# Splits of weights through a PSUM bank, one bank less for layer 2, and one quadrant kept in PSUM

## The chip, the cores and the metric

The kernel runs on one core of one Trainium2 chip. The metric is device time in microseconds of one execution; the kernel before was timed in three runs. The engines are named as in the profile: PE (TensorE, matmuls), PEld (its weight loads), DVE (VectorE), ACT (ScalarE), POOL (GpSimd), SP (SyncE, which issues most DMAs).

## The reference, cut to what matters

```
x = retention(q, k, v)            # scores * decay mask, times v; 4 x 576 tokens = 2304, 512 wide
for e in range(4):                # first mixture: every token through every expert
    out1 += p[:, e] * (relu(x @ w1[e]) @ w2[e])        # w1: 512x1024, w2: 1024x512
e_idx = argmax(out1 @ w_gate)     # second mixture: one of 8 experts per token
out[t] = gate[t] * sigmoid(out1[t] @ w_output_gate)[e_idx] * (relu(out1[t] @ w1s[e_idx]) @ w2s[e_idx])
```

All matrix products are done with pairs of float16 numbers: each float32 operand is split into `hi` (the float16 value) and `lo` (what is left, also as float16), and three products hi·hi, hi·lo, lo·hi are summed in PSUM.

## The kernel before, in words

**Splitting.** `split(raw, hi, lo, scale)` (lines 191 to 193) makes such a pair from a float32 tile in SBUF: ACT writes `hi` from `raw` (L192), then DVE computes `raw*scale - hi` into `lo` (L193). DVE so reads two tiles in SBUF, `raw` and `hi`. Three kinds of tiles go through it in the middle of the program: the first mixture's weights of experts 1 to 3 (`put`, tiles `wr` to `wm_a`, `wm_b`, `wm_c`), the staged pieces of the second mixture's weights (`s_split`, tiles `sr` to `s`, written back to DRAM for later), and rows of the result for the gate (`g1_rows`, tile `xr`). The splits of the opening and those whose source is already in PSUM use the same function.

**Expert 0** (`e = 0`, 18 to 268 us of the trace): nine blocks of 256 tokens. In a block, four units of layer 1 (`l1_first`, PSUM tag `h`) and four of layer 2 (`l2`, PSUM tag `o`) run, with steps of the retention (`at_hook`) and one staged piece (`s_hook`) between them. `x_keep` splits mixed token tiles at the end of a block: `hi` by ACT (L349), `lo` by DVE (L350).

**Experts 1 to 3** (268 to 816 us) use a product scheme with seven instead of eight quarter products (matrices cut in quadrants and mixed first). A block has seven layer-1 units (products 1, 5, 6, 2, 3, 7, 4; 24 matmuls each, L523) that alternate with seven layer-2 units of the block before it (12 matmuls each, L608). The mixing of the weights is done by POOL (`mix`, L438), each mixed quarter is then split by `put`; the lower halves `lo` of the mixed activations are done by POOL too (L542).

In layer 1, PSUM banks `x` (tag `h`), `y` and `q` hold running sums. Product 5 is copied from `q` to an SBUF tile `s5` by ACT (L564); later DVE adds a running sum to it in place (L583, in `m7`), and this tile is the source of two mixes (L546) and of the quadrant "22" (`keep`, L481 and L482). In the traces' names the tile `s5` is shown as `s`.

In layer 2, products 1, 6, 7 and 4 go through one bank `X` (tag `x2`), each followed by an `add` on DVE into the accumulator `acc` (L616, `acc<-px`). Products 1 and 6 are summed on top of each other in `X`, as are all four: unit 6 can start only after the `add` of unit 1 has read `X`. Product 5 starts a second bank `v` (`acc<-pv` 128x256), which 2 and 3 then fill. The order of the products is the list `ORDER2`. Before, `X` has two buffers and `v` is taken from the pool `ps_o` (tag `o`), so a block's `X` doesn't wait for the block before.

**What sets the order on an engine.** Each engine works off its own list in order. The lists are made by a scheduler when the program is built, from the order of the code and its own estimate; `tc.issue_after` keeps a split behind the last `keep`. `w_plan` says after which units a weight step is done and `s_plan` after which units a staged piece.

The last stage (816 to 1042 us) is the second mixture: gathered rows, matmuls of L1019 and L1036, scattered rows.

Of the kernel before, what the change touches and what calls it, by code (L numbers as in the profile page):

```python
# [43 lines left out]
HOOKS = {0: 1, 2: 1}, {0: 1, 2: 1, 3: 1, 5: 1}  # L44
W1_AT = {24: 0, 25: 2, 26: 1, 27: 3}
ORDER1 = (1, 5, 6, 2, 3, 7, 4)
ORDER2 = (1, 5, 6, 2, 7, 3, 4)
W1_POS = (
    {2: ("a", 8), 0: ("a", 9), 1: ("a", 10), 3: ("a", 11), 5: ("c", 0), 4: ("c", 1), 6: ("c", 2)},
    {c: ("a", c) for c in range(7)},  # L50
# [79 lines left out]
def kernel(  # L130
# [60 lines left out]
    def split(raw, hi, lo, scale):  # L191
        act.activation(out=hi, in_=raw, func=ACTF.Copy, scale=scale)  # L192
        dve.scalar_tensor_tensor(out=lo, in0=raw, scalar=scale, in1=hi, op0=ALU.mult, op1=ALU.subtract)  # L193

    def w_parts(r, first, second):
        for i in range(2):
# [148 lines left out]
    def x_keep(b):  # L345
        m = xfs.pop(b)
        for i in range(2):
            hi, lo = [xcs[b][:, a, 4 + 2 * i:6 + 2 * i] for a in range(2)]
            act.activation(out=hi, in_=m[:, i], func=ACTF.Copy)  # L349
            dve.tensor_tensor(out=lo, in0=m[:, i], in1=hi, op=ALU.subtract)  # L350
        dst = xcd[b * 128:(b + 1) * 128]
        sp.dma_start(out=dst[:, :, 0:2], in_=xcs[b][:, :, 0:2])
        pace["sp"] = sp.dma_start(out=dst[:, :, 3:], in_=xcs[b][:, :, 3:])
# [75 lines left out]
    def put(e, n, k, i, c):  # L429
        t = wt[e][n][c]  # L430
        if n:
            t = t[:, 2 * k:2 * k + 2]
            split(quarter(e, n, k, i), t[:, :, 0], t[:, :, 1], S_W)
        else:
            split(quarter(e, n, k, i), t[:, k, 0], t[:, k, 1], S_W)

    def mix(e, n, k, to, x, y, op):
        pace["pool"] = pool.tensor_tensor(out=quarter(e, n, k, to), in0=quarter(e, n, k, x), in1=quarter(e, n, k, y), op=op)  # L438
# [71 lines left out]
    def l1_mixed(e, b):  # L510
# [49 lines left out]
        def m5():  # L560
            q = t["q"] = bank("q", later["mix"])
            mm(q, 5, True)
            t["s"] = sb("s5", 2)
            act.activation(out=t["s"], in_=q, func=ACTF.Copy)  # L564

        def m6():
# [12 lines left out]

        def m7():  # L580
            mm(t["x"], 7)
            s5 = t["s"]
            dve.tensor_tensor(out=s5, in0=t["x"], in1=s5, op=ALU.add)  # L583
            mixed("s1", s5, t["r"], ALU.add)
            mixed("s2", s5, t["s3"], ALU.subtract)
            keep(s5, op_of("22"))

        def m4():
            mm(t["x"], 4)
# [6 lines left out]
    def l2_mixed(e, b):  # L596

        o, w = ops[e, b], wt[e][1]
        t = {}
        X = later["mix"].tile([128, 512], F32, tag="x2", name="px2", bufs=2)[:, 0:256]  # L600
        names = {1: ("11", 0), 5: ("s1", 1), 6: ("s2", 2), 2: ("12", 3), 7: ("s3", 4), 3: ("s4", 5), 4: ("22", 6)}

        def mm(out, m, first):
            a, c = names[m]
            n = 0
            for k in range(4):
                for u, v in TERMS:
                    pe.matmul(  # L608
                        out, lhsT=o[a][:, v, k], rhs=w[c][:, k, u], start=(first and n == 0), stop=(n == 11),
                        skip_group_check=True,  # L610
                    )
                    n += 1

        def add(i, c0, c1, src):
            a = acc[:, b * TB + i, c0:c1]
            dve.scalar_tensor_tensor(  # L616
                out=a, in0=src, scalar=p_sb[:, b * TB + i, e:e + 1], in1=a, op0=ALU.mult, op1=ALU.add
            )

        def go(m):  # L620
            if m in (1, 6, 7, 4):
                mm(X, m, m == 1)
                add({1: 0, 6: 0, 7: 1, 4: 1}[m], *{1: (0, 256), 6: (256, 512), 7: (256, 512), 4: (0, 256)}[m], X)
            elif m == 5:
                t["v"] = ps_o[0].tile([128, 2, 256], F32, tag="o", name="pv")
                mm(t["v"][:, 1], 5, True)
                add(1, 256, 512, t["v"][:, 1])
            elif m == 2:
                mm(t["v"][:, 0], 2, False)
            else:  # L630
                mm(t["v"][:, 1], 3, False)
                add(0, 0, 512, t["v"].rearrange("p a d -> p (a d)"))

        return [lambda m=m: go(m) for m in ORDER2]

# [34 lines left out]
    def s_split(i):  # L670
        e, j = divmod(i, 16)
        t = s16_p.tile([128, 2, 512], F16, tag="s16", name="s16")
        split(stage.pop(i), t[:, 0], t[:, 1], S_W)
        if j < 8:
            k, c = divmod(j, 2)
            return w1d[e * 128:(e + 1) * 128, k, :, 512 * c:512 * c + 512], t
        return w2d[e * 128:(e + 1) * 128, j - 8], t
# [28 lines left out]
    def g1_rows(t, pl):  # L706

        xr = pl.tile([128, 2, DM], F16, tag="xr", name="xr")
        split(acc[:, t, 0:DM], xr[:, 0], xr[:, 1], S_X1)
        x1h[t] = xr  # L710

    def g1_turn(t, pl):
# [487 lines left out]

    def s_plan(e, b, u):
        if e == 0:
            if 1 <= b < 8:
                s_hook()
        elif b >= 2 or (e, b) == (1, 1):
            if u in ((1, 5, 8) if b % 2 else (1, 3, 6, 8)):
                s_hook()
        elif b == 1 and u in (6, 8):
            s_hook()
# [38 lines left out]
    for e in range(E1):  # L1248
        for b in range(NB + (e == E1 - 1)):
# [11 lines left out]
                gp.append(ctx.enter_context(tc.tile_pool(name="gp", bufs=2)))  # L1261
            for u, unit in enumerate(units):
                unit()
                if (e, b, u) == (0, NB - 1, 0):
                    with tc.issue_after(pace["sp"].ins):
                        x_load(0, sp)
# [137 lines left out]
```

## Time and profile before

| | us |
|---|---|
| median of 3 runs (lowest, highest) | 1045.91 (1044.99, 1050.87) |
| profiled execution, its own time | 1044.05 |
| span of its trace, first to last instruction | 1042.2 |
| PE busy in the span | 984.2 |
| DVE busy | 616.8 |
| ACT busy | 394.2 |
| POOL busy | 391.5 |

The table is read from the top: the profiled execution has its own time, and what is worked out from its trace is set against that; the span is 1.85 us shorter. PE is busy 94% of the span, so what other engines do matters where PE waits for them. The program has stages with different loads; a mean over the whole span hides that.

### The profile page before, as it was taken

The numbers are of one execution on the slowest core, as the hardware profiler recorded it, in microseconds if no ns is written. First come the engines' busy times: TensorE is split into PE (matmuls) and PEld (weight loads), VectorE is DVE, ScalarE is ACT, GpSimd is POOL, SyncE is SP. The second block draws the span as 40 slices with busy tenths as digits, with TensorE's granted clock in tenths as the row PEclk, the third lists the DMA queues.
The fourth block names the chain that finished last, engine by engine and source line by source line (L and its number), as shares of the span: only waits on it lengthen the run. The fifth ranks groups of instructions, "written<-read, shape, count | busy, mean of one in ns | idle before, by whom it ended". The sixth has DMA issues, their size and how long they took to land. (4 is left out here: it accounts for less than half of the span.)

```text
span 1042.2 us, 30436 instructions
## 1 busy us (share of the span) xinstructions
PE 984.2 (94%) x13075; PEld 819.2 (79%) x13075; DVE 616.8 (59%) x1171; ACT 394.2 (38%) x729; POOL 391.5 (38%) x391
## 2 busy tenths in 40 slices
PE   6899999899998999899899999999999999999995
PEld 5566666566798999899899998898888677777773
DVE  5455444675767877866877687888877512112111
ACT  4234333544533544444445354434432222222221
POOL 3433333644435544533544373423423121121211
PEclk9999999999999999989999999999999999999998
DMA  9778887668363655535464622687436425372691
GB/s 349 215 243 273 266 272 255 222 196 275 121 183 115 178 171 165 148 117 158 120 211 138 204 86 78 177 188 205 128 77 226 175 108 211 125 299 80 262 393 73
DMA packets 94956, 195.10 MB, mean 187 GB/s; under 512 B 21278, under 2 KB 42782, under 8 KB 91744
## 3 DMA queue, kind: packets, MB, share of 16 engines
q1 hardware_dynamic: 84400, 154.35, 44.7%
q0 software_dynamic: 10416, 38.76, 12.3%
q8 instruction: 104, 1.70, 0.7%
q14 instruction: 36, 0.29, 0.1%
HBM read 184.78 MB, written 51.81 MB: 227 GB/s over the span
## 5 line engine op out<-in xcount | busy, mean ns | idle before, releaser
L608 PEld LDWEIGHTS <-op 128*128 128x128 f16 x2268 | 216.0, 99 | 35.6 <-POOL wr L438 10.0
L542 POOL TENSOR_TENSOR op<-sm,op 128x512 f16<-128x512 f32 x108 | 141.9, 1324 | 247.8 <-ACT op L541 244.7
L523 PEld LDWEIGHTS <-wm_a 128*128 128x128 f16 x2592 | 155.3, 98 | 11.9 <-issue 9.0
L193 DVE SCALAR_TENSOR_TENSOR s<-sr,s 128x512 f16<-128x512 f32 x128 | 110.4, 874 | 33.9 <-ACT s L192 33.6
L1029 DVE SCALAR_TENSOR_TENSOR h_s<-p_h,h_s 128x512 f16<-128x512 f32 x40 | 27.6, 690 | 158.4 <-ACT h_s L1028 158.4
L1019 PEld LDWEIGHTS <-wm_a 128*128 128x128 f16 x1920 | 108.9, 98 | 4.2
L1019 PE MATMUL p_h<-x_s,wm_a 128*128 128x128 f16 x1920 | 110.9, 219 | 0.0
L495 PE MATMUL ph<-xc,wm_a 128*128 128x256 f16 (+1 forms) x960 | 101.9, 264 | 8.6 <-POOL xc L335 4.1
L541 ACT ACTIVATE op<-sm 128x512 f16<-128x512 f32 x108 | 67.2, 629 | 100.2 <-DVE sm L546 100.2
L495 PEld LDWEIGHTS <-wm_a 128*128 128x128 f16 x960 | 86.0, 99 | 21.2 <-issue 9.9
L523 PE MATMUL ph<-xc,wm_a 128*128 128x128 f16 x1512 | 94.8, 219 | 8.3 <-DVE s L583 8.3
L646 PE MATMUL po<-wm_a,ht 128*128 128x512 f16 x432 | 96.4, 379 | 1.1 <-DVE xf L331 1.1
L192 ACT ACTIVATE s<-sr 128x512 f16<-128x512 f32 x128 | 77.5, 622 | 47.2 <-DMA w1d<-s 22.7
L438 POOL TENSOR_TENSOR wr<-wr 128x512 f32<-128x512 f32 x48 | 71.5, 1501 | 45.3 <-DVE wm_a L193 29.0
L1036 PEld LDWEIGHTS <-h_s 128*128 128x128 f16 x480 | 46.7, 98 | 52.3 <-DVE h_s L1029 0.7
L1036 PE MATMUL p_y<-wm_b,h_s 128*128 128x512 f16 x372 | 83.9, 379 | 0.5 <-DVE h_s L1029 0.5
L608 PE MATMUL px<-wm_a,op 128*128 128x256 f16 x648 | 79.7, 272 | 2.8 <-DVE acc L616 2.8
L646 PEld LDWEIGHTS <-ht 128*128 128x128 f16 x432 | 40.9, 98 | 49.1 <-DVE xf L331 1.3
L523 PEld LDWEIGHTS <-wm_b 128*128 128x128 f16 x1296 | 76.7, 98 | 1.2
L1039 POOL DMA_INDIRECT out_dram<-y_s,sidxm x17 | 17.3, 1018 | 146.8 <-ACT y_s L1038 138.1
L193 DVE SCALAR_TENSOR_TENSOR wm_a<-wr,wm_a 128x512 f16<-128x512 f32 x62 | 68.0, 1119 | 0.1
L608 PE MATMUL pv<-wm_a,op 128*128 128x256 f16 x540 | 66.5, 273 | 1.2 <-DVE xs L193 0.6
(185 smaller groups left out, 1473.4 us busy)
## 6 DMA issues: line engine op xcount, KB each, us to landing
wm_a<-w1d SPq DMA_DIRECT2D x20, 2048.0 KB
wm_b<-w2d SPq DMA_DIRECT2D x10, 2048.0 KB
wr<-in_w_dram SPq DMA_DIRECT2D x32, 512.0 KB
sr<-in_w1s_dram SPq DMA_DIRECT2D x64, 256.0 KB
w1d<-s SPq DMA_DIRECT2D x64, 256.0 KB
sr<-in_w2s_dram SPq DMA_DIRECT2D x64, 256.0 KB
w2d<-s SPq DMA_DIRECT2D x64, 256.0 KB
xc<-xcd POOLq DMA_DIRECT2D x25, 640.0 KB, 6.1
```

Of the source, the lines that this page charges most:

```text
L192: act.activation(out=hi, in_=raw, func=ACTF.Copy, scale=scale)
L193: dve.scalar_tensor_tensor(out=lo, in0=raw, scalar=scale, in1=hi, op0=ALU.mult, op1=ALU.subtract)
L438: pace["pool"] = pool.tensor_tensor(out=quarter(e, n, k, to), in0=quarter(e, n, k, x), in1=quarter(e, n, k, y), op=op)
L495: pe.matmul(ph[:, i, h0:h1], lhsT=w[:, k, u, f * 128:(f + 1) * 128], rhs=x[:, v, k // 2 + 2 * h0:k // 2 + 2 * h1 - 1:2, k % 2], start=(n = ...
L523: pe.matmul(bank[:, i], lhsT=w[:, k, u, 128 * i:128 * i + 128], rhs=x[:, v, d, k], start=(first and i == 0 and n == 0), stop=(n == 5), ski ...
L541: act.activation(out=hi, in_=s, func=ACTF.Copy)
L542: pool.tensor_tensor(out=lo, in0=s, in1=hi, op=ALU.subtract)
L608: pe.matmul(out, lhsT=o[a][:, v, k], rhs=w[c][:, k, u], start=(first and n == 0), stop=(n == 11), skip_group_check=True,)
L646: pe.matmul(po, lhsT=hts[k // 2][:, x, k % 2, i * 128:(i + 1) * 128], rhs=w[:, k, y], start=(k == 0 and n == 0), stop=(k == KF - 1 and n = ...
L1019: pe.matmul(ph[:, j], lhsT=w[k][:, x, f * 128:(f + 1) * 128], rhs=xs[:, y, k], start=(n == 0), stop=(n == 3 * KD - 1),)
L1029: dve.scalar_tensor_tensor(out=lo, in0=ph, scalar=0.0, in1=hi, op0=ALU.max, op1=ALU.subtract)
L1036: pe.matmul(po, lhsT=h[:, a, k], rhs=w[k][:, b], start=(n == 0), stop=(n == 3 * KF - 1))
```

## The change

Splits of weights, staged pieces and gate rows get a new function `split_z`: ACT copies the scaled source to a bank in PSUM, ACT writes `hi` from that bank, and DVE subtracts `hi` from the bank. That is one more instruction on ACT for each of 224 splits (by the lists of instructions); DVE's instruction now reads one tile in PSUM and one in SBUF. The bank is taken from tag `o` or, in expert 0 behind the layer-1 units, from tag `h`. For that, layer 2 frees a bank: `X` has one buffer, `v` one of its own, and `ORDER2` starts with 5 instead of 1. The sum of `m7` is written to the bank `q` instead of to `s5`, which becomes single. `x_keep`'s subtraction moves from DVE to POOL. `s_plan` puts seven instead of eight pieces in a block of expert 0, and four in every later block instead of three and four by turns.

```
-ORDER2 = (1, 5, 6, 2, 7, 3, 4)
+ORDER2 = (5, 1, 6, 2, 7, 3, 4)
...
+    def split_z(raw, hi, lo, scale):
+        z = z_at["bank"]().tile([128, 512], F32, tag=z_at["tag"], name="pz")
+        if len(raw.shape) == 3:
+            z = z.rearrange("p (k d) -> p k d", k=raw.shape[1])
+        act.activation(out=z, in_=raw, func=ACTF.Copy, scale=scale)
+        act.activation(out=hi, in_=z, func=ACTF.Copy)
+        dve.tensor_tensor(out=lo, in0=z, in1=hi, op=ALU.subtract)
+
+    def z_from(first):
+        z_at["bank"], z_at["tag"] = ((lambda: ps), "h") if first else ((lambda: ps_o[0]), "o")
...
             act.activation(out=hi, in_=m[:, i], func=ACTF.Copy)
-            dve.tensor_tensor(out=lo, in0=m[:, i], in1=hi, op=ALU.subtract)
+            pool.tensor_tensor(out=lo, in0=m[:, i], in1=hi, op=ALU.subtract)
...
-            split(quarter(e, n, k, i), t[:, :, 0], t[:, :, 1], S_W)
+            split_z(quarter(e, n, k, i), t[:, :, 0], t[:, :, 1], S_W)
         else:
-            split(quarter(e, n, k, i), t[:, k, 0], t[:, k, 1], S_W)
+            split_z(quarter(e, n, k, i), t[:, k, 0], t[:, k, 1], S_W)
...
-            t["s"] = sb("s5", 2)
+            t["s"] = sb("s5", 1)
...
             mm(t["x"], 7)
-            s5 = t["s"]
-            dve.tensor_tensor(out=s5, in0=t["x"], in1=s5, op=ALU.add)
-            mixed("s1", s5, t["r"], ALU.add)
-            mixed("s2", s5, t["s3"], ALU.subtract)
-            keep(s5, op_of("22"))
+            q = t["q"]
+            dve.tensor_tensor(out=q, in0=t["x"], in1=t["s"], op=ALU.add)
+            mixed("s1", q, t["r"], ALU.add)
+            mixed("s2", q, t["s3"], ALU.subtract)
+            keep(q, op_of("22"))
...
-        X = later["mix"].tile([128, 512], F32, tag="x2", name="px2", bufs=2)[:, 0:256]
+        X = later["mix"].tile([128, 512], F32, tag="x2", name="px2")[:, 0:256]
...
-                t["v"] = ps_o[0].tile([128, 2, 256], F32, tag="o", name="pv")
+                t["v"] = later["mix"].tile([128, 2, 256], F32, tag="v", name="pv")
...
-        split(stage.pop(i), t[:, 0], t[:, 1], S_W)
+        split_z(stage.pop(i), t[:, 0], t[:, 1], S_W)
...
-        split(acc[:, t, 0:DM], xr[:, 0], xr[:, 1], S_X1)
+        split_z(acc[:, t, 0:DM], xr[:, 0], xr[:, 1], S_X1)
...
         if e == 0:
-            if 1 <= b < 8:
+            if 1 <= b < 8 and u < 7:
                 s_hook()
         elif b >= 2 or (e, b) == (1, 1):
-            if u in ((1, 5, 8) if b % 2 else (1, 3, 6, 8)):
+            if u in (1, 3, 6, 8):
                 s_hook()
...
                 unit()
+                z_from(e == 0 and (b == 0 or u >= 4))
```

**First place: DVE, start of expert 2's first block.** These are DVE's rows before, from the `add` of layer-2 unit 4 of one block to the `add` of unit 6 of the next; `px` with a new number is the new block's `X`.

```order
L616 SCALAR_TENSOR_TENSOR acc<-px_6519,p_sb,acc 128x256
L193 SCALAR_TENSOR_TENSOR wm_c<-wr,wm_c 128x2x256 x2
L193 SCALAR_TENSOR_TENSOR wm_a<-wr,wm_a 128x2x256
L616 SCALAR_TENSOR_TENSOR acc<-px_6855,p_sb,acc 128x256
L193 SCALAR_TENSOR_TENSOR wm_a<-wr,wm_a 128x2x256 x3
L616 SCALAR_TENSOR_TENSOR acc<-pv,p_sb,acc 128x256
L568 TENSOR_TENSOR pq<-ph,s_6930 128x512
L616 SCALAR_TENSOR_TENSOR acc<-px_6855,p_sb,acc 128x256
```

And these are the same stretch of DVE's list in the changed kernel.

```order
L629 SCALAR_TENSOR_TENSOR acc<-px_6735,p_sb,acc 128x256
L203 TENSOR_TENSOR wm_c<-pz,wm_c 128x2x256
L629 SCALAR_TENSOR_TENSOR acc<-pv,p_sb,acc 128x256
L203 TENSOR_TENSOR wm_c<-pz,wm_c 128x2x256
L203 TENSOR_TENSOR wm_a<-pz,wm_a 128x2x256
L629 SCALAR_TENSOR_TENSOR acc<-px_7083,p_sb,acc 128x256
L203 TENSOR_TENSOR wm_a<-pz,wm_a 128x2x256 x2
L581 TENSOR_TENSOR pq<-ph,s_7163 128x512
L203 TENSOR_TENSOR wm_a<-pz,wm_a 128x2x256
L629 SCALAR_TENSOR_TENSOR acc<-px_7083,p_sb,acc 128x256
```

The weight subtractions now read `pz`; the `add` of `pv` (product 5) comes first, and that of `px` (product 1), for which unit 6 waits, is second. Between the two adds stand two subtractions where there were three.

**Second place: ACT, expert 1's fifth block.** Before, ACT's list from the `hi` of quadrant "22" to the copy of product 5:

```order
L481 ACTIVATE op<-s_5274 128x512
L481 ACTIVATE op<-ph 128x512
L192 ACTIVATE wm_a<-wr 128x512
L192 ACTIVATE s_5578<-sr 128x512
L192 ACTIVATE wm_a<-wr 128x512
L192 ACTIVATE s_5666<-sr 128x512
L541 ACTIVATE op<-sm 128x512
L558 ACTIVATE py<-ph 128x512
L564 ACTIVATE s_5606<-pq 128x512
```

In the changed kernel, expert 1's fifth block, from and to the same two:

```order
L494 ACTIVATE op<-pq 128x512
L201 ACTIVATE pz<-wr 128x512
L494 ACTIVATE op<-ph 128x512
L202 ACTIVATE wm_a<-pz 128x512
L201 ACTIVATE pz<-sr 128x512
L202 ACTIVATE s_5399<-pz 128x512
L201 ACTIVATE pz<-wr 128x512
L571 ACTIVATE py<-ph 128x512
L554 ACTIVATE op<-sm 128x512
L202 ACTIVATE wm_a<-pz 128x512
L201 ACTIVATE pz<-sr 128x512
L202 ACTIVATE s_5451<-pz 128x512
L577 ACTIVATE s_5429<-pq 128x512
```

Each `hi` has a copy to `pz` ahead of it, and four more instructions stand between the two ends.

**Third place: DVE in a block of expert 3, where the gate's small work runs too.** Before, from the `add` of product 4 of one block to that of product 5 of the next (`xr` is a gate row, `s_` a staged piece; `ri`, `pp`, `tq` and `ohp` are the gate's):

```order
L616 SCALAR_TENSOR_TENSOR acc<-px_11272,p_sb,acc 128x256
L773 TENSOR_SCALAR ri<-ri 128x2
L193 SCALAR_TENSOR_TENSOR xr<-acc,xr 128x512
L775 TENSOR_TENSOR pp<-ri 128x2
L776 CAST tq<-ri 128x2
L193 SCALAR_TENSOR_TENSOR s_11720<-sr,s_11720 128x512
L777 TENSOR_TENSOR ohp<-kb,pp 128x256
L616 SCALAR_TENSOR_TENSOR acc<-px_11670,p_sb,acc 128x256
L193 SCALAR_TENSOR_TENSOR xr<-acc,xr 128x512
L193 SCALAR_TENSOR_TENSOR s_11812<-sr,s_11812 128x512
L616 SCALAR_TENSOR_TENSOR acc<-pv,p_sb,acc 128x256
```

In the changed kernel, such a block from the `add` of product 4 to that of product 1:

```order
L629 SCALAR_TENSOR_TENSOR acc<-px_11692,p_sb,acc 128x256
L786 TENSOR_SCALAR ri<-ri 128x2
L203 TENSOR_TENSOR xr<-pz,xr 128x512
L788 TENSOR_TENSOR pp<-ri 128x2
L789 CAST tq<-ri 128x2
L203 TENSOR_TENSOR s_12155<-pz,s_12155 128x512
L790 TENSOR_TENSOR ohp<-kb,pp 128x256
L629 SCALAR_TENSOR_TENSOR acc<-pv,p_sb,acc 128x256
L203 TENSOR_TENSOR xr<-pz,xr 128x512
L203 TENSOR_TENSOR s_12212<-pz,s_12212 128x512
L629 SCALAR_TENSOR_TENSOR acc<-px_12102,p_sb,acc 128x256
```

Nothing but the two adds has changed places: product 5's `add` now has the earlier one and product 1's, for which unit 6 waits, the later one.

## Rows read from the trace of the kernel before

**Rows 1.** The page: busy time, share of the span and instructions of each engine.

```profile
PE 984.2 (94%) x13075; PEld 819.2 (79%) x13075; DVE 616.8 (59%) x1171; ACT 394.2 (38%) x729; POOL 391.5 (38%) x391
```

**Rows 2.** Busy time by stage: experts 1 and 2, then expert 3.

```profile
core 0: us, PE busy (x) PEld busy (x) DVE busy (x) ACT busy (x) POOL busy (x), PEclk, DMA share, GB/s
268.00:652.00 384.00, 370.30 (x4974) 348.86 (x4973) 287.50 (x411) 175.86 (x318) 176.97 (x149) 0.98 0.48 147
652.00:816.00 164.00, 154.67 (x2138) 143.97 (x2136) 135.24 (x412) 62.87 (x126) 55.74 (x53) 1.00 0.57 160
```

**Rows 3.** PE's waits, 268 to 652 us: total, times, longest.

```profile
PE px L608 <- DVE acc L616: 10.4, 4, 4.0
PE ph L523 <- DVE s L583: 2.8, 2, 2.4
```

**Rows 4.** Timeline around the longest wait: start, us, engine, instructions.

```profile
437.28 5.40 DVE L193 SCALAR_TENSOR_TENSOR wm_a<-wr,wm_a 128x512 f16<-128x512 f32 x1
437.32 1.16 POOL L542 TENSOR_TENSOR op<-sm,op 128x512 f16<-128x512 f32 x1
438.44 3.70 POOL L438 TENSOR_TENSOR wr<-wr 128x512 f32<-128x512 f32 x3
442.61 0.47 DVE L616 SCALAR_TENSOR_TENSOR acc<-px,p_sb,acc 128x256 f32<-128x256 f32 x1
443.13 0.37 PE L608 MATMUL px<-wm_b,op 128*128 128x256 f16 x1 [4.00 <-DVE acc L616]
```

**Rows 5.** Stretches behind three waits, columns as in rows 2.

```profile
326.00:329.00 3.00, 3.00 (x17) 2.20 (x17) 1.19 (x3) 0.00 (x0) 0.00 (x0) 0.50 0.74 231
442.00:448.50 6.50, 5.37 (x38) 4.51 (x38) 4.37 (x8) 0.00 (x0) 2.94 (x3) 0.50 0.00 0
630.00:633.00 3.00, 3.00 (x19) 2.33 (x18) 2.45 (x5) 3.00 (x7) 2.52 (x2) 0.50 0.00 0
```

**Rows 6.** Groups of instructions, 268 to 652 us: busy, mean ns of one.

```profile
L193 DVE SCALAR_TENSOR_TENSOR s<-sr,s 128x512 f16<-128x512 f32 x57 | 55.3, 989 | 0.9 <-ACT s L192 0.7
L193 DVE SCALAR_TENSOR_TENSOR wm_a<-wr,wm_a 128x512 f16<-128x512 f32 x38 | 46.4, 1246 | 0.1
L568 DVE TENSOR_TENSOR pq<-ph,s 128x512 f32<-128x512 f32 x20 | 13.9, 693 | 13.4 <-PE ph L523 13.4
L192 ACT ACTIVATE s<-sr 128x512 f16<-128x512 f32 x58 | 34.5, 619 | 1.3 <-DVE s L193 0.9 <-DVE op L482 0.2 <-DMA w2d<-s 0.2
L558 ACT ACTIVATE py<-ph 128x512 f32<-128x512 f32 x20 | 11.6, 579 | 0.9 <-PE py L556 0.9
```

**Rows 7.** Timeline of expert 1's fifth block, ACT, PE and DVE.

```profile
338.32 0.61 ACT L481 ACTIVATE op<-s 128x512 f16<-128x512 f32 x1
338.84 0.61 ACT L192 ACTIVATE wm_a<-wr 128x512 f16<-128x512 f32 x1
...
344.72 1.50 PE L523 MATMUL ph<-xc,wm_c 128*128 128x128 f16 x24
...
345.90 0.47 DVE L616 SCALAR_TENSOR_TENSOR acc<-pv,p_sb,acc 128x256 f32<-128x256 f32 x1
346.06 1.47 PE L608 MATMUL px<-wm_b,op 128*128 128x256 f16 x12
```

**Rows 8.** Timeline of expert 3, first and last of four alike blocks.

```profile
678.88 1.47 PE L608 MATMUL px<-wm_a,op 128*128 128x256 f16 x12
679.86 0.47 DVE L616 SCALAR_TENSOR_TENSOR acc<-pv,p_sb,acc 128x256 f32<-128x256 f32 x1
...
739.27 1.47 PE L608 MATMUL px<-wm_a,op 128*128 128x256 f16 x12
740.24 0.47 DVE L616 SCALAR_TENSOR_TENSOR acc<-pv,p_sb,acc 128x256 f32<-128x256 f32 x1
```

**Rows 9.** PE's waits, 18 to 268 us: total, times, longest.

```profile
PE ph L495 <- POOL xc L335: 4.1, 5, 1.0
PE uo L270 <- DVE xf L331: 2.3, 1, 2.3
```

More of the change, by code (lines that the diff above doesn't have):

```diff
@@ L193, in split @@
         dve.scalar_tensor_tensor(out=lo, in0=raw, scalar=scale, in1=hi, op0=ALU.mult, op1=ALU.subtract)
+    z_at = {}
+    def split_z(raw, hi, lo, scale):
[7 more added lines that the diff above has]
+        z_at["bank"], z_at["tag"] = ((lambda: ps), "h") if first else ((lambda: ps_o[0]), "o")
     def w_parts(r, first, second):
```

## The prediction

> **What bounds the kernel now.** I read the page first, then the stages, then who waits for whom, then the timeline of the longest waits. PE is busy 94% of the span [rows 1], so the kernel is bound by its matmuls, and a change that touches no matmul can only win back PE's waits and what they bring with them. Per stage, experts 1 and 2 leave PE 384.00 - 370.30 = 13.7 us idle and expert 3 leaves 9.3 [rows 2]. In experts 1 and 2 nearly all of it is two groups [rows 3]: layer-2 units that wait for an `add` (10.4 us in four waits) and layer-1 units that wait for the sum of product 7 (2.8 us in two).
>
> The longest of the four shows what is late [rows 4]. DVE works on one `lo` of a weight split for 5.40 us, while POOL runs four instructions end to end, from 437.32 to 442.14. DVE's instruction ends half a microsecond after POOL's last. Behind it stands the `add` of product 1, and for that PE waits 4.00 us. The same split takes 1.25 us in the mean and a staged piece's 0.99, where a subtraction of DVE with one source in PSUM takes 0.69 [rows 6]. So what is slow is DVE's reading of two SBUF tiles beside a busy POOL.
>
> A wait costs more than itself. Behind three of them the granted clock is 0.50 (1.2 instead of 2.4 GHz) for 3.0, 6.5 and 3.0 us [rows 5]; in 12.5 us at half clock PE loses 6.3 us. What can be won in this stage is therefore 10.4 + 2.8 + 6.3 = 19.5 us.
>
> **The change, part by part.** *DVE's instruction.* 224 subtractions (128 staged pieces, 84 weights, 12 gate rows, counted in the lists) go from two SBUF sources to one in PSUM and one in SBUF. Before doesn't show that exact form; the nearest row is the running sum in `q` at 0.69 us, the others lie at 0.99 and 1.25 [rows 6]. I take 0.69: 57 x (0.99 - 0.69) + 38 x (1.25 - 0.69) = 38 us of 287.5 in experts 1 and 2 [rows 2, 6], and above all no more instruction of 5 us. PE's wait for the `add` behind it goes.
>
> *ACT's extra instruction.* Nothing shows an ACT copy from SBUF to PSUM; from PSUM to PSUM it takes 0.58 and from SBUF to SBUF 0.62 [rows 6], and ACT starts one every 0.52 us [rows 7]. I take 0.52 of queue and 0.6 of latency. 224 of them are 117 to 139 us on an ACT that is busy 176 of 384 us [rows 2], off PE's path as a sum. As a chain it counts: a split now takes two instructions before DVE can start, and copy, `hi` and subtraction stand in front of what PE waits for. In the fifth block of expert 1 four more stand between quadrant "22" and the copy of product 5 (second place), 2.1 us.
>
> *One `X` and the new order.* Before, three units lie between product 1 and unit 6, which needs the `add` of product 1. Now one does: the `add` must be over within one layer-1 unit, 346.06 - 344.72 = 1.34 us [rows 7]. With 0.47 for the `add`, some 0.8 us remain. What before's `add` of product 5 met at that place is what product 1's meets now. In the fifth block of expert 1 it ran from 345.90 to 346.37, 0.3 us past the unit's start [rows 7]; its splits, now shorter, win that back and ACT's longer chain gives it away. I take 0.1 us for each of some 16 such blocks, 1.6, with 0 and 0.5 as ends. That `X` and `v` are single costs nothing: four units lie between their last reader and next writer, and `add`s run 1 to 3 us behind.
>
> *Bursts.* At the start of experts 2 and 3 a weight step follows every unit. Copy and `hi` make 1.1 us per step on ACT, where a unit takes 1.34 [rows 7], so ACT, with its other work, falls behind. Two subtractions at ACT's pace, 2.2 us, lie between the adds of 5 and 1 (first place); product 1's unit ends two units, 2.6 us, after product 5's, so with DVE 1 us behind the `add` ends 0.5 us late. Further on the copy of product 3 comes late in the same way, and with it the sum of 7, by 1.2. I leave 1.7 for each of two bursts and 1 for the beginning of expert 1: 4.4, with 0 and 10 as ends (nothing, and half of today's 19.5).
>
> *Expert 3.* Here the exchange costs. In four alike blocks DVE starts the `add` of product 5 0.98 us after unit 6 has started [rows 8]: harmless, as unit 6 doesn't wait for it. Now product 1's `add` stands in that place, behind the same gate row and staged piece (third place), and unit 6 waits until it ends: 0.98 + 0.47 = 1.45, with the signal 1.5 us. Three of these blocks carry both pieces in the changed list, one a piece less (0.9): 5.4 us. Ends: 0, if DVE is earlier there, and 9, if ACT's second instruction delays the row too.
>
> *Expert 0.* One wait there, 2.3 us, is for a step behind slow splits [rows 9]; it goes. The five for POOL's `xc`, 4.1 us, stay. In two blocks weights and pieces share tag `o` with layer 2's sums: a copy, a `hi` and a subtraction, twice, are some 3.3 us (4 x 0.52, 0.6 and 0.69) against a retention step and part of a unit, so I take 1.1 us each. Together nothing, with -4 and +4 as ends. `x_keep`'s 18 subtractions cost POOL some 1.2 us each and free DVE of 0.69; nobody waits for them at once. The sum in `q` frees DVE a little more; `q` must be free 6 units later. Both at nothing.
>
> The sum against the profiled execution's 1044.05: -19.5 + 1.6 + 4.4 + 5.4 + 0 = -8.1, so 1036. The runs shown have a median 1.9 above it; I set 1036.5 between the two, against the median 1045.91 a change of -0.9%.
>
> **A rule weighed.** DVE's 5.40 us span four POOL instructions [rows 4]. The Trainium skill ("SBUF — State Buffer", Who interferes with whom) says that a DVE instruction with two SBUF inputs and a GpSimd instruction that reads SBUF share a port pair, that whoever comes first holds it for its whole instruction, and that the other is blocked till then. By that DVE would be let in after the first of the four, at 438.48; the trace says 442.14. If only that first instruction were the port's doing, a wait would lose about 1.2 of its 4.00 us with the change and the rest would stay: the rule's way is the rival "only part is the port" below.
>
> **The rivals.** *A: everything goes, expert 3 isn't hurt.* Splits in expert 3 come early enough, bursts run free: 1044.05 - 19.5 - 2.3 + 1.6 = 1024. For it speaks that DVE has less to do; against it that expert 3's DVE, busy 135 of 164 us [rows 2], keeps its gate work.
>
> *B: the waits change places.* The win is real but product 1's `add`, the bursts and expert 3 take it back: 9 for expert 3, 10 for bursts, 16 x 0.3 = 4.8: 1044.05 - 19.5 + 23.8 = 1048 at the far end, 1043 in its middle. *Only part is the port* (0.05 of B's chance): POOL's first instruction alone holds DVE, something else the rest; three waits lose 1.2 each, no half clock goes, 1044 - 3.6 + 5.4 = 1046. Against it: the end of DVE's instruction follows POOL's last [rows 4].
>
> *C: ACT's chain sets the pace (slower).* If a block's last `lo` before product 1's `add` comes one ACT instruction and one subtraction later than I reckon (0.6 + 0.7), unit 6 waits some 0.9 us in every one of 21 blocks with pieces: 19 us, and with expert 3's 5.4 and the bursts' 4.4 the sum is 1044.05 - 19.5 + 28.8 = 1053. It decides from 0.8 us of lateness, the room in rows 7. Half-clock stretches behind such waits would add to it. Against it: ACT was busy 176 of 384 us there, and the 95 splits of rows 6 add 95 x 0.52 = 49 us, 59% in all.
>
> **How the numbers follow.** The forecast, 1029 to 1041, has 0.55; A (1020 to 1029) 0.13; B (1041 to 1049) 0.20; C (above 1049) 0.12. Half a per cent, 5.2 us, is about what a measurement can tell from no change. Faster by more, below 1040.7: 0.13 + 0.53 = 0.66. Within: 0.22, of B and the forecast's edge. Slower: 0.12. The range leaves out the far ends of A and C: 1025 to 1049.
>
> **What would show it.** In the changed kernel's profile: DVE's subtractions from `pz` at 0.69 us with no instruction of 5 us; no wait of 2 to 4 us in experts 1 and 2 and no stretch at clock 0.5 there; PE's waits for `acc<-px` many and short, about 1.5 us each in expert 3, all at unit 6; ACT busy some 510 to 530 us. The forecast is wrong if unit 6 waits in most blocks of experts 1 and 2 (C), if expert 3 shows no such wait (A), or if subtractions from PSUM are still stretched beside POOL (part of B).

## The result and the profile after

The changed kernel takes 1029.2 us in the median (1028.64 to 1031.16, 4 runs), against 1045.45 of the kernel before in the same set. The ratio is 0.984, 95% interval [0.980, 0.988]. In a second set of runs it was 0.986 [0.983, 0.989]. So it is 1.2 to 2.0% faster by the first interval: the side was forecast, the size was not (16 us instead of 9). 1029.2 lies 0.2 us inside the lower end of the range, the second set's 1032.4 lies 3.4 us inside.

The page of the profiled execution (1028.75 us, span 1027.0), the line that answers to [rows 1]:

```profile
PE 980.8 (96%) x13075; PEld 816.5 (80%) x13075; DVE 543.8 (53%) x1153; ACT 504.3 (49%) x953; POOL 375.7 (37%) x409
```

PE has the same 13075 matmuls and 3.4 us less busy time. ACT gained 110 us of work, and DVE lost 73, of which 40.0 in experts 1 and 2 (287.50 to 247.50), where 38 were reckoned. By stage, over the same work as [rows 2] (the stages end earlier now):

```profile
core 0: us, PE busy (x) PEld busy (x) DVE busy (x) ACT busy (x) POOL busy (x), PEclk, DMA share, GB/s
266.00:633.40 367.40, 364.00 (x4965) 344.18 (x4963) 247.50 (x420) 238.55 (x452) 156.72 (x150) 1.00 0.51 164
633.40:801.00 167.60, 155.52 (x2137) 143.81 (x2135) 131.38 (x411) 79.01 (x155) 50.46 (x52) 1.00 0.57 157
```

Experts 1 and 2 took 384.0 us and take 367.4. PE's idle time there fell from 13.7 to 3.4 us, and its busy time by 6.3 us: the three stretches at half clock [rows 5] are gone (PEclk 1.00, not 0.98). Expert 3 became longer, from 164.0 to 167.6. PE's waits, in total, times and longest, first in experts 1 and 2 (where [rows 3] had 10.4 and 2.8), then in expert 3:

```profile
PE ph L536 <- DVE pq L596: 1.9, 3, 0.8
PE pv L621 <- POOL op L555: 0.8, 1, 0.8
...
PE pg L737 <- DMA xs<-xr: 3.0, 6, 0.7
PE ph L536 <- DVE pq L596: 2.8, 4, 0.8
PE px L621 <- DVE acc L629: 2.2, 3, 0.7
PE ph L536 <- DVE acc L809: 1.7, 2, 0.9
```

The start of expert 2, the place of [rows 4], now looks like this:

```profile
432.22 4.95 POOL L451 TENSOR_TENSOR wr<-wr 128x512 f32<-128x512 f32 x4
432.36 0.47 DVE L629 SCALAR_TENSOR_TENSOR acc<-px,p_sb,acc 128x256 f32<-128x256 f32 x1
433.25 0.69 DVE L203 TENSOR_TENSOR wm_a<-pz,wm_a 128x512 f16<-128x512 f32 x1 [0.41 <-ACT wm_a L202]
434.37 0.69 DVE L203 TENSOR_TENSOR wm_a<-pz,wm_a 128x512 f16<-128x512 f32 x1 [0.43 <-ACT wm_a L202]
435.57 0.68 DVE L203 TENSOR_TENSOR wm_a<-pz,wm_a 128x512 f16<-128x512 f32 x1
```

POOL runs four mixes end to end for 4.95 us, and beside them DVE makes three `lo` at 0.69 us each. Where one stood for 5.40 us, none is held. DVE now waits 0.4 us for ACT's `hi`, which costs PE nothing here.

For where the time went I use four marks that every run has: the second block of expert 0's layer-2 matmuls (`po`, M), the first matmul of product 2 (`py`) in expert 1's first block (A), in expert 3's third (B) and in its last (C). They are starts in the timeline.

| us | to M | M to A, expert 0 | A to B, experts 1, 2, start of 3 | B to C, expert 3 | C to end |
|---|---|---|---|---|---|
| before | 42.5 | 229.9 | 386.8 | 124.4 | 258.6 |
| after | 44.6 | 225.7 | 370.2 | 128.5 | 258.0 |
| difference | +2.1 | -4.2 | -16.5 | +4.1 | -0.6 |
| forecast | 0 | 0 | -13.5 | +5.4 | 0 |

### The profile page after: what moved, and what is told of

The parts are those of the page before. It is cut to its first block, busy times and chain, and to the rows that moved or that the text cites. A ratio compares the mean times of both kernels' runs of the same rounds, so it can differ in the third digit from the quotient of the medians.

```text
span 1027.0 us, 30806 instructions
## 1 busy us (share of the span) xinstructions
PE 980.8 (96%) x13075; PEld 816.5 (80%) x13075; DVE 543.8 (53%) x1153; ACT 504.3 (49%) x953; POOL 375.7 (37%) x409
## 5 line engine op out<-in xcount | busy, mean ns | idle before, releaser
L555 POOL TENSOR_TENSOR op<-sm,op 128x512 f16<-128x512 f32 x108 | 123.9, 1156 | 283.8 <-ACT op L554 283.2
L203 DVE TENSOR_TENSOR s<-pz,s 128x512 f16<-128x512 f32 x128 | 86.5, 687 | 54.4 <-ACT s L202 53.5
L201 ACT ACTIVATE pz<-sr 128x512 f32<-128x512 f32 x128 | 75.3, 600 | 18.1 <-DMA sr<-in_w1s_dram 7.8
L202 ACT ACTIVATE s<-pz 128x512 f16<-128x512 f32 x128 | 74.4, 597 | 11.3 <-DMA w2d<-s 7.2
L1052 POOL DMA_INDIRECT out_dram<-y_s,sidxm x17 | 17.2, 1013 | 146.8 <-ACT y_s L1051 138.2
L451 POOL TENSOR_TENSOR wr<-wr 128x512 f32<-128x512 f32 x48 | 60.4, 1269 | 28.1 <-ACT pz L201 27.4
```

The source lines that it names most:

```text
L201: act.activation(out=z, in_=raw, func=ACTF.Copy, scale=scale)
L202: act.activation(out=hi, in_=z, func=ACTF.Copy)
L203: dve.tensor_tensor(out=lo, in0=z, in1=hi, op=ALU.subtract)
L555: pool.tensor_tensor(out=lo, in0=s, in1=hi, op=ALU.subtract)
```

## The experiments

The main theory, "reading": DVE's instruction with two SBUF sources is held while POOL works, so PE waits and its clock halves; the gain is that DVE reads PSUM. The main rival, "order": the gain comes from what else was changed. All times are medians, ratios are to the kernel before on the same chip.

| run | us | ratio, 95% interval | M to A | A to B | B to C |
|---|---|---|---|---|---|
| changed, again | 1032.4 | 0.986 [0.983, 0.989] | 226.3 | 370.2 | 131.8 |
| e1 two SBUF sources | 1044.6 | 0.999 [0.997, 1.000] | 227.3 | 387.4 | 125.5 |
| e11 z in SBUF | 1052.7 | 1.008 [1.005, 1.010] | 224.9 | 392.7 | 132.9 |
| e2 before, short mixes | 1059.6 | see there | 234.8 | 367.3 | 124.4 |
| e10 before, half mixes | 1039.8 | 0.994 [0.993, 0.996] | 233.4 | 377.0 | 124.5 |
| e3 product 1 first | 1047.9 | 1.002 [1.000, 1.003] | 226.2 | 383.5 | 136.3 |
| e4 eight pieces | 1031.0 | 0.984 [0.982, 0.987] | 229.4 | 370.2 | 125.5 |
| e5 x_keep on DVE | 1030.2 | 0.984 [0.981, 0.987] | 225.6 | 370.2 | 129.3 |
| e6 late direct | 1027.2 | 0.983 [0.978, 0.987] | 225.5 | 370.2 | 125.9 |
| e7 two between | 1025.6 | 0.979 [0.976, 0.982] | 225.4 | 369.7 | 125.8 |
| e8 both | 1021.8 | 0.977 [0.975, 0.979] | 227.9 | 369.7 | 122.8 |
| e9 all | 1021.1 | 0.976 [0.973, 0.978] | 225.1 | 369.7 | 122.2 |

### e1: the changed kernel, reading undone

```diff
-            split_z(quarter(e, n, k, i), t[:, k, 0], t[:, k, 1], S_W)
+            split(quarter(e, n, k, i), t[:, k, 0], t[:, k, 1], S_W)
```

and the same in the other three calls.

> The changed kernel with only the reading undone: weights, pieces and gate rows are split straight from SBUF again; order, banks, places of the pieces and x_keep stay as changed. Theory 'reading' (the gain comes from DVE no longer reading two SBUF tiles beside POOL's weight mixes): the lo of wm_a is back at about 1.2 us in the mean with some of 4 us and more, PE waits of 2 to 4 us and stretches at clock 0.5 are back in experts 1 and 2, the landmarks there lose some 14 us, and the time is 1041 to 1050 us. Rival 'order' (the gain comes from product 5 ahead of 1, from where the pieces lie or from x_keep on POOL): DVE is slow again but PE does not wait, and the time stays at 1028 to 1033.

1044.6 us: the whole gain is gone with the reading. In its trace, start of expert 2 and PE's waits from 265 to 640 us:

```profile
435.97 5.02 DVE L193 SCALAR_TENSOR_TENSOR wm_a<-wr,wm_a 128x512 f16<-128x512 f32 x1
436.74 3.70 POOL L451 TENSOR_TENSOR wr<-wr 128x512 f32<-128x512 f32 x3
...
PE px L621 <- DVE acc L629: 14.2, 5, 4.9
```

"Reading" is right and "order" falls. It leaves one question: this run has no second instruction on ACT either.

### e11: the same two instructions on ACT, z in SBUF

`z` is taken from an SBUF pool of two buffers instead of the PSUM tags (two buffers each as well), from the end of expert 0 to the end of expert 3's first block (the lines that open and close that pool are left out here).

```diff
-                z_from(e == 0 and (b == 0 or u >= 4))
+                z_from(e == 0 and (b == 0 or u >= 4)); z_at.update(dict(bank=lambda: z_p[0], tag='z') if 0 < e < 3 or (e, b) == (3, 0) and u < 13 else {})
```

> The changed kernel in which the copy z lies in SBUF instead of PSUM through experts 1 and 2 and the first block of expert 3; ACT does its two instructions and DVE its subtraction as changed, so DVE reads two SBUF tiles again and only the place of z differs. Theory 'reading': the subtractions there are back above 1 us in the mean with some of 3 us and more, PE waits of 2 to 4 us and half-clock stretches are back, the stretch from the first block of expert 1 to the first of expert 3 takes 385 us or more instead of 370, and the time is 1042 to 1052 us. Rival 'two steps on ACT' (the gain comes from ACT handing DVE its work later and more spread out, wherever z lies): DVE's instructions may be longer but PE does not wait, 1028 to 1034.

1052.7 us, 0.7 past the upper end of the theory's range, and A to B takes 392.7, 22.4 more than with `z` in PSUM. The mean of `wm_a` is 1.12 us, and PE waits 15.4 us in eleven times for the `add` (270 to 650 us). Only one `lo` takes more than 1.8 us, and it is the longest of all; behind it stands 6.3 us of the 15.4, the other ten waits come with `lo` of 1.8 us at most. The timeline of the long one, start of expert 3, and behind it a window with the columns of [rows 2]:

```profile
612.62 6.14 POOL L451 TENSOR_TENSOR wr<-wr 128x512 f32<-128x512 f32 x5
612.85 6.46 DVE L203 TENSOR_TENSOR wm_a<-pz,wm_a 128x512 f16<-128x512 f32 x1 [0.82 <-ACT wm_a L202]
...
619.00:625.00 6.00, 4.64 (x37) 3.85 (x37) 3.69 (x7) 2.27 (x4) 0.00 (x0) 0.54 0.00 0
```

POOL's five mixes end at 618.76, DVE's instruction at 619.31, and behind PE's wait of 6.3 us the granted clock is near half. With ACT's second instruction in place and only the tile moved, the gain turns into a loss, so it is the place of `z` that pays.

### e2: the kernel before, POOL's mixes on 8 of 512 columns

The rest of each quarter is left unmixed. The lists of PE, DVE and ACT are unchanged, instruction by instruction.

```diff
-        pace["pool"] = pool.tensor_tensor(out=quarter(e, n, k, to), in0=quarter(e, n, k, x), in1=quarter(e, n, k, y), op=op)
+        f = lambda i: quarter(e, n, k, i)[:, :, 0:4] if n else quarter(e, n, k, i)[:, 0:8]; pace["pool"] = pool.tensor_tensor(out=f(to), in0=f(x), in1=f(y), op=op)
```

> The kernel before, in which each of POOL's weight mixes works on 8 of 512 columns and leaves the rest of the quarter unmixed; every engine's list of instructions is the same otherwise. Theory 'reading': with nothing long on POOL to hold it, DVE's lo of wm_a falls from 1.25 us to 0.7 to 0.9 in experts 1 and 2, none takes over 2 us, the three stretches at clock 0.5 go, and the time is 1025 to 1031 us. Rival 'DVE is slow by itself' (two SBUF sources and a multiplication cost it the time whatever POOL does): wm_a stays above 1.1 us and the time at 1042 to 1046. Rival 'only one instruction is held': DVE gains 1.2 us per wait, half clock stays in part, about 1038 to 1041.

The time, 1059.6 us, doesn't compare: with other numbers the tokens go to other experts, and the last stage has 372 matmuls more (C to the end 290.0 us, not 258.6). Up to C it does. A to B takes 367.3 us instead of 386.8, 19.5 less, what the forecast called the most that can be won there (that the two agree to a tenth is chance, as 1.2 us of waits are left). Its windows A to B, its PE waits (265 to 640 us) and two groups (270 to 640 us):

```profile
277.70:645.00 367.30, 366.11 (x4996) 347.41 (x4994) 273.58 (x418) 176.54 (x320) 147.43 (x152) 1.00 0.51 155
...
PE px L608 <- DVE acc L616: 0.8, 1, 0.8
...
L193 DVE SCALAR_TENSOR_TENSOR wm_a<-wr,wm_a 128x512 f16<-128x512 f32 x38 | 35.5, 962 | 0.0
L438 POOL TENSOR_TENSOR wr<-wr 128x8 f32<-128x8 f32 x32 | 14.5, 460 | 40.6 <-DVE wm_a L193 28.4 <-DVE wm_b L193 11.5
```

PE is idle 1.2 us of 367, at full clock. DVE's `lo` is still slow (0.96 us, more than the 0.7 to 0.9 expected; each one over 0.8 us stands beside an `op` of POOL, which remain), but none of a weight or piece is over 2.05 us. PE waited for what stood beside POOL's chains of full-length mixes, not for the mean. Expert 0 lost 4.9 us here for another reason, below.

### e10: the kernel before, each mix in two halves

```diff
-        pace["pool"] = pool.tensor_tensor(out=quarter(e, n, k, to), in0=quarter(e, n, k, x), in1=quarter(e, n, k, y), op=op)
+        h = [(lambda i, s=s: quarter(e, n, k, i)[:, s:s + 1] if n else quarter(e, n, k, i)[:, 256 * s:256 * s + 256]) for s in range(2)]; pace["pool"] = [pool.tensor_tensor(out=f(to), in0=f(x), in1=f(y), op=op) for f in h][-1]
```

> The kernel before, in which each weight mix on POOL is two instructions of half the columns, end to end. Theory 'held until POOL pauses': DVE's lo beside such a chain is held as long as before, wm_a stays above 1.1 us in the mean with instructions of 3 to 5 us, the waits of 2 to 4 us and the half-clock stretches stay, 1041 to 1050 us. Rival 'held for one instruction': DVE comes in after half a mix (some 0.7 us), no lo takes over 2 us, and the time falls to 1028 to 1036.

1039.8 us, below the first theory's range and above the rival's: neither. The instructions say more. The timeline of expert 2, POOL's rows and DVE's at two places:

```profile
494.04 3.18 DVE L193 SCALAR_TENSOR_TENSOR s<-sr,s 128x512 f16<-128x512 f32 x1
494.08 0.72 POOL L381 DMA_DIRECT2D xc<-xcd  x1
494.83 1.16 POOL L542 TENSOR_TENSOR op<-sm,op 128x512 f16<-128x512 f32 x1
...
495.94 3.68 POOL L438 TENSOR_TENSOR wr<-wr 128x256 f32<-128x256 f32 x4
...
438.62 3.52 DVE L193 SCALAR_TENSOR_TENSOR wm_a<-wr,wm_a 128x512 f16<-128x512 f32 x3
439.28 3.43 POOL L438 TENSOR_TENSOR wr<-wr 128x256 f32<-128x256 f32 x3
```

DVE's first instruction ends at 497.22, 2.4 us ahead of POOL's last half (499.62). If its own work took the usual 0.68 us, it was let in at 496.5, half a us after `op` had ended, while POOL's chain went on; so it is not always held until POOL pauses. At the second place three `lo` and three halves go side by side, at 1.2 us each, by turns. DVE and ACT work off the same lists as before; both kinds of places occur in one run, so the time alone decides nothing.

### e3 and e7: the order of layer 2's products

```diff
-ORDER2 = (5, 1, 6, 2, 7, 3, 4)
+ORDER2 = (1, 5, 6, 2, 7, 3, 4)
```

> The changed kernel with product 1 ahead of 5 again, X still in one bank. Theory 'one unit of room' (unit 6 waits in expert 3 because only one layer-1 unit lies between it and product 1): the three waits of 0.9 us at unit 6 go; what waits now is product 1 for the add of product 4 of the block before, again with one unit between, but behind less DVE work: at most 0.3 us in a regular block. Expert 3 gains 2 to 3 us, the time is 1026 to 1028. Rival 'it moves to the block's start': product 1 waits about 0.5 us or more in every block of experts 1 to 3, and the time is 1034 to 1045.

The rival is right, past its upper end: 1047.9 us. Unit 1 now follows the block before's product 4 in the one `X`, and waits in nearly every block of experts 1 and 2 (270 to 655 us):

```profile
PE px L621 <- DVE acc L629: 11.0, 18, 1.2
```

Moving product 5 ahead of 1 is therefore what makes one `X` affordable. With four products in `X` and seven places, one pair must stand next to each other; e7 puts it at 6 and 7.

```diff
-ORDER2 = (5, 1, 6, 2, 7, 3, 4)
+ORDER2 = (5, 1, 2, 6, 7, 3, 4)
```

> The changed kernel with the layer-2 products in the order 5, 1, 2, 6, 7, 3, 4: product 2, which doesn't use X, stands between 1 and 6, and the pair that follows each other in X with one layer-1 unit between is now 6 and 7. Theory 'DVE is free there': the add of 6 follows the lo of quadrant 11 and is done 0.4 to 0.6 us ahead of unit 7; the three waits of 0.9 us at unit 6 in expert 3 go and the time is 1025.5 to 1027.5 us. Rival 'the wait moves': unit 7 waits 0.3 us or more in most blocks, as unit 1 did with product 1 first, and the time is 1032 to 1045.

1025.6 us as expected: DVE is free between 6 and 7, and PE's list of waits in expert 3 has no `px` any more. B to C falls from 128.5 (131.8 in the second trace) to 125.8.

### e6, e8, e9: expert 3's rows, and all together

```diff
-        split_z(stage.pop(i), t[:, 0], t[:, 1], S_W)
+        (split if late3[0] else split_z)(stage.pop(i), t[:, 0], t[:, 1], S_W)
...
-        split_z(acc[:, t, 0:DM], xr[:, 0], xr[:, 1], S_X1)
+        split(acc[:, t, 0:DM], xr[:, 0], xr[:, 1], S_X1)
```

`late3[0]` is true in expert 3 from its third block on.

> The changed kernel in which expert 3, from its third block on, splits gate rows and staged pieces straight from SBUF (there POOL has no weight mixes). Theory 'ACT's second instruction delays the row' (my far end for expert 3): the gate row is ready 0.6 us or more earlier, PE's waits for the turned rows (xs, six, 3.0 us) mostly go and expert 3 gains 2 to 4 us: 1025 to 1027. Rival 'only the order counts': the subtractions of row and piece still stand ahead of product 1's add, unit 6 waits 0.9 us three times as before, the rows' waits stay, and the time is 1028 to 1031.

1027.2 us; the interval overlaps that of the changed kernel's second set, so the trace has to tell. PE's waits in expert 3, of this kernel (640 to 768 us):

```profile
PE ph L536 <- DVE acc L809: 5.6, 6, 1.2
PE px L621 <- DVE acc L629: 2.7, 4, 0.8
```

And one of before (652 to 785 us):

```profile
PE ph L523 <- DVE s L583: 5.5, 6, 1.4
```

The first line is unit 4's wait behind product 7 (put down to a small write of DVE just after the sum), which before has too, 5.5 us in six times. The waits for turned rows, `pg<-xs`, are gone (3.0 us in the first trace of the changed kernel, 6.3 in the second), those at unit 6 remain.

The theory's reason is wrong all the same: the row isn't ready earlier. In each of the three blocks with such waits the first row's `lo` ends 8.1 us before PE is free for the turned row in the changed kernel, and 8.0 us here. What moved is a DMA on POOL's list, the store `x1d<-acc` of finished rows. This is one block, in the changed kernel and then in this one:

```profile
653.54 0.73 POOL L812 DMA_DIRECT2D x1d<-acc  x1
656.11 1.24 SPq L727 DMA_TRANSPOSE xs<-xr  x1
...
650.87 0.73 POOL L812 DMA_DIRECT2D x1d<-acc  x1 [2.04 <-DVE acc L809]
656.83 1.24 SPq L727 DMA_TRANSPOSE xs<-xr  x1
```

The store is issued 2.6 us ahead of the row's turn in the one and 6.0 us in the other. So it is in all traces: where it is 1.3 to 2.6 us ahead in these three blocks (both traces of the changed kernel, e3, e5, e7, e11), PE waits 3.0 to 6.8 us for the turned rows, where it is 6.0 or more (before, e1, e2, e6, e8, e9, e10) 0.5 at most. In e4, whose rows go through PSUM like the changed kernel's, it is 2.6, 2.9 and 6.0 us ahead, and all 1.8 us of waits are in the first of the three. So ACT's second instruction doesn't make the turned row late by its own time. That the store's transfers do is read from the traces and not tested: no run moves the store alone, nor shows why the scheduler put it there. The order alone and this edit together:

> The changed kernel with both edits that won something: layer-2 products in the order 5, 1, 2, 6, 7, 3, 4 and gate rows and staged pieces of expert 3, from its third block on, split straight from SBUF. The first took the three waits at unit 6 (2.7 us), the second the waits for the turned gate rows (3 to 5 us in the runs). If they are separate they add up: expert 3 gains about 6 us against the changed kernel, 1020 to 1023 us. Rival 'one wait hides the other' (taking either lets the other grow): no better than the order alone, 1024 to 1027.

1021.8 us: they add up, B to C is 122.8, below the 124.4 of before. With `x_keep` on DVE besides (e9, its edit is e5's):

> The run with both edits, and x_keep's subtractions on DVE again, which won 1.0 us of the opening between its steps of the retention. If that holds beside the others, 0.5 to 1 us less than the run with both; rival: expert 0 gives it back, the same time within 0.5 us.

1021.1 us, 0.7 less; the intervals overlap, so that last step is not told from none. Of all these kernels it is the fastest, 8 and 11 us below the changed one's two medians.

### e4, e5 and the changed kernel again: expert 0 and the opening

```diff
-            if 1 <= b < 8 and u < 7:
+            if 1 <= b < 8:
```

> The changed kernel with eight staged pieces in a block of expert 0, as before. Theory 'the eighth piece' (expert 0 gained because the lo of the block's last piece no longer stands between pf and xf at the block's border): waits of layer-1 units for xc of 0.7 to 1.8 us come back at three to five borders, expert 0 loses 2 to 4 us, the time is 1031 to 1033. Rival 'reading' for this part too (expert 0 gained because its late blocks hold weight mixes that held DVE): expert 0 keeps its 4.5 us and the time stays within 1 us of 1029.

1031.0 us, not told from the changed kernel. Inside it is: expert 0 loses 3.7 us (225.7 to 229.4), all but 0.5 of what it had gained, and its waits for POOL's `xc` are back, 2.4 us in four times. e1, which reads two SBUF tiles again, keeps 2.6 us of the gain, so reading is at most a part of it. Expert 3 wins 3.0 (128.5 to 125.5; the two traces of the changed kernel differ by 3.3 there, so the size is loose): by the lists it has 8 pieces left instead of 15. Why a piece costs in expert 0 shows in the timeline of before at a block's border:

```profile
183.40 0.63 ACT L192 ACTIVATE s<-sr 128x512 f16<-128x512 f32 x1 [3.35 <-DMA w1d<-s]
184.06 0.69 DVE L193 SCALAR_TENSOR_TENSOR s<-sr,s 128x512 f16<-128x512 f32 x1 [3.60 <-ACT s L192]
...
185.38 0.69 DVE L193 SCALAR_TENSOR_TENSOR s<-sr,s 128x512 f16<-128x512 f32 x1 [0.29 <-ACT s L192]
...
186.32 0.41 DVE L331 TENSOR_TENSOR xf<-uo,ka 128x256 f32<-128x256 f32 x1
...
187.24 0.27 PE L495 MATMUL ph<-xc,wm_a 128*128 128x256 f16 x1 [0.52 <-ACT xc L333]
...
188.46 0.82 PE L495 MATMUL ph<-xc,wm_a 128*128 128x256 f16 x6 [0.95 <-POOL xc L335]
```

A piece's buffer is free only when its store has landed; ACT waits 3.35 us for that, DVE's `lo` waits for ACT, and `xf`, which the next block needs, stands behind it and the next piece's `lo` on DVE; PE then waits 0.52 and 0.95 us. In e2 the same wait was 4.7 us, and PE lost 3.0 there.

```diff
-            pool.tensor_tensor(out=lo, in0=m[:, i], in1=hi, op=ALU.subtract)
+            dve.tensor_tensor(out=lo, in0=m[:, i], in1=hi, op=ALU.subtract)
```

> The changed kernel with x_keep's 18 subtractions on DVE again. Theory 'nothing' (nobody waits for them at once): 1028 to 1031 us, expert 0 within 1 us of the changed kernel. Rival 'part of expert 0's gain' (an lo less on DVE at each block's border lets pf and xf go earlier): expert 0 loses 1 to 3 us, 1030 to 1032. Rival 'the opening' (two subtractions on POOL delay the first tokens): the opening wins 1.5 to 2 us, 1027.

1030.2 us, the same; "nothing" holds, also for expert 0 (225.6). The opening doesn't get its 2 us back (M at 43.6).

> The changed kernel once more, beside the other runs of this group. 1028 to 1031 us. Its opening shows whether the 2 us that the changed kernel is behind at its first layer-2 units (39.8 and 44.6 us against 38.3 and 42.5) come back: if the change causes them they do, if they are the chance of the first loads they come out otherwise.

1032.4 us; M at 43.4. In the eleven traces of the changed kernel and of those built from it M lies between 43.0 and 45.0, in before, e2 and e10 between 41.9 and 42.9. So the opening seems to pay some 1.6 us (the means are 44.1 and 42.4); for which edit no run tells.

## Why the prediction was right, and by how much it was off

**What bounds the kernel: right.** A stretched `lo`, the `add` behind it, PE's wait and the half clock after it are one chain. (The stretch at 630 us [rows 5] stands behind the sum of product 7 and four slowed `lo`, shown at the end.) e2 took POOL's chains away and won 19.5 us in A to B, the sum of [rows 3, 5]; e1 and e11 put the two SBUF sources back and lost 17.2 and 22.4.

**DVE's instruction: right.** 0.69 us was taken; it is 686 ns in experts 1 and 2, for pieces and weights alike:

```profile
L203 DVE TENSOR_TENSOR s<-pz,s 128x512 f16<-128x512 f32 x64 | 42.8, 686 | 19.6 <-ACT s L202 19.6
L201 ACT ACTIVATE pz<-sr 128x512 f32<-128x512 f32 x65 | 37.9, 601 | 1.9 <-DVE s L203 1.1 <-DVE wm_a L203 0.5 <-DVE wm_b L203 0.3
```

ACT's extra instruction was taken at 0.6 us latency and takes 0.60; ACT's 504 us lie just under the 510 to 530 forecast.

**One `X` and the new order: smaller still.** 1.6 us were set for 16 blocks. e7, which takes the wait away, shortens A to B by 0.5, so it is 0.03 us a block. That the order itself is worth 13 us there (e3) the prediction didn't see.

**Bursts: mis-sized.** 4.4 us were set. At unit 6 nothing waited at the starts of experts 2 and 3; the sum of product 7 was late, as said, by 0.6 us in the mean (1.9 us in three waits) and not 1.2. What is left in A to B against e2 is 370.2 - 367.3 = 2.9 us, for bursts and regular blocks together, where 6.0 were reckoned. Of the 7 us by which the forecast was short, A to B is 3.0, expert 0 is 4.2, expert 3 is 1.3 and the end 0.6, less 2.1 lost in the opening.

**Expert 3: right in place, wrong in make-up.** The waits for product 1's `add` are there, three, all at unit 6, at 0.74 us and not 1.5:

```profile
658.24 0.67 DVE L203 TENSOR_TENSOR xr<-pz,xr 128x512 f16<-128x512 f32 x1
...
658.88 0.69 DVE L203 TENSOR_TENSOR s<-pz,s 128x512 f16<-128x512 f32 x1
...
659.49 0.48 DVE L629 SCALAR_TENSOR_TENSOR acc<-px,p_sb,acc 128x256 f32<-128x256 f32 x1
...
660.02 1.47 PE L621 MATMUL px<-wm_a,op 128*128 128x256 f16 x12 [0.74 <-DVE acc L629]
```

The `add` does stand behind row and piece. But unit 6 could have started at 660.02 - 0.74 = 659.28, so the `add` began 0.2 us late and not the 0.98 read from [rows 8]: DVE was through with its row sooner. In turn the turned rows come late to PE (`pg<-xs`, 3.0 us), which the prediction had only as a far end and put down to ACT; e6 shows the rows no later and a store nearer to them. These two are 5.2 us, less 1.0 that unit 4 waits less behind product 7 (1.7 + 2.8 us instead of 5.5): about the 4.1 measured. That 5.4 came near is luck in part, and the second trace of the changed kernel, 3.3 us longer there with 6.3 us of waits for rows, shows how loose this term is.

**Expert 0: the step that failed.** "Together nothing" and "The five for POOL's `xc`, 4.1 us, stay" were wrong: 4.2 us were won and the five waits fell to one of 0.6. `s_plan`'s seventh piece instead of an eighth was in the change and had no term. e4 puts it at 3.7 of the 4.2 us. Expert 3 didn't pay for it: by the lists of instructions the seven pieces went to A to B (66 instead of 59, under the new plan of four in every block), and B to C has 15 before and after. What they cost in A to B no run shows alone; it is within the 2.9 us left there. The wait of 2.3 us for slow splits fell to 0.9, not to nothing; in e1 it is 2.3 again.

**The rule weighed.** The row decided rightly that the whole 5.40 us were POOL's doing: e2 took only POOL's time away, and the waits went. As a general law "until POOL's last" falls with e10. The Trainium skill ("SBUF — State Buffer", Who interferes with whom) says that a DVE instruction with at most one SBUF input, outside its 2-port modes, does not contend with GpSimd; the trace agrees, with 0.69 us beside four mixes. The Trainium skill ("SBUF — State Buffer", SBUF: two separate sides) has the first comer hold the pair for its whole instruction and the other blocked; by that DVE would come in after one mix, and 6.46 us through five (e11) say otherwise. [rows 4] was a poor place to weigh this: DVE's row there begins 0.04 us ahead of POOL's (437.28 and 437.32), so that it isn't clear who came second; in e11 POOL is clearly first (612.62 and 612.85).

**The rivals.** A's 1024 needed expert 3 unhurt; e8 shows that this was to be had, with another order and other rows. B and C did not happen at their size: the one stage in which waits changed places is expert 3, at 4.1 us, and ACT at 65% of experts 1 and 2 (238.55 of 367.40) set no pace.

## What to carry to other kernels

Look at the longest instructions of a group and at rows of slowed ones, not at its mean: with 0.96 us in the mean PE lost next to nothing (e2), one `lo` of 5.4 us cost 4 us and the clock, and in e11 `lo` of at most 1.8 us came with 9.1 us of waits. When a bank is saved, ask between which two users of the one left the shortest stretch lies, and put that pair where the engine that empties the bank is idle. An edit of the plan that only moves work from one stage to another has a term in both; count the instructions of each stage before saying which one pays.

## What the runs showed that was not expected

POOL gains as well when DVE reads PSUM: its `op` fell from 1324 to 1156 ns in the mean and its weight mixes from 1501 to 1269, over the whole span.

Which of the two comes in is not settled. DVE was held through three whole mixes (before, e1) and through five (e11). In other places the two took turns, with half mixes (e10) and with whole ones too. This is before at the start of expert 3:

```profile
619.85 6.30 POOL L438 TENSOR_TENSOR wr<-wr 128x512 f32<-128x512 f32 x4
620.66 6.04 DVE L193 SCALAR_TENSOR_TENSOR wm_a<-wr,wm_a 128x512 f16<-128x512 f32 x4
```

Four `lo` and four mixes take 1.5 and 1.6 us each in the mean, where a `lo` alone takes 0.68; behind them PE waits 2.4 us for the sum of product 7 [rows 3], and the clock is halved at 630 us [rows 5]. So "held until POOL's last" fails in the trace of before as well. POOL's instructions stood end to end in both kinds of places. What decides between them was not found.

A DMA issue on POOL plays a part, but by itself it holds nothing. In before, 18 split subtractions between 268 and 660 us began beside an issue with POOL's next computing instruction over 0.9 us behind: all took 0.68 us. With that instruction 0.3 to 0.7 us behind, 8 of 17 that began beside an issue took 2.0 to 3.6 us; of 18 in the whole trace that began with POOL idle and its next instruction 0.3 to 0.8 us behind, none took over 0.7. The `lo` of 494.04 in e10 is one of those held: it began 0.8 us ahead of POOL's `op`, beside the issue of L381, and 0.68 us would have been enough to be done before it.
